# Third layer of a two-block feed-forward kernel with seven block products in place of eight, work moved between POOL, DVE and ACT, weights decoded ahead, inputs laid out as tiles

## The chip, the cores and the metric

The kernel runs on one core of one Trainium2 chip, as one program with one launch. The metric is the device time of that core in microseconds (us), the median of several executions. How the inputs are laid out on the host before the launch is not part of the time.

## The reference

```
x   = attention(q, k, v, cap)            # 4 batches, 12 heads, 448 tokens, head size 64
                                         # scores = cap * tanh(q k^T / 8 / cap), softmax over keys, times v
x   = x as (1792, 768)                   # 4 batches of 448 rows, 12 heads side by side
h   = max(x @ w1, x @ w2, x @ w3)        # layer 1: three 768 x 768 matrices
y   = h @ w_out                          # layer 2: 768 x 768
u   = sigmoid(y @ w_gate) * (y @ w_val)  # layer 3: two 768 x 1536 matrices
out = u @ w_out2                         # layer 4: 1536 x 768
```

The weights reach the kernel as 64-bit floats. The kernel rebuilds 32-bit floats from the two halves of each number ("decoding").

## The kernel before

**Precision.** A product of two 32-bit matrices is made of three TensorE passes: each factor is split into a high part (a cast to fp32r) and a low part (the factor less its high part), and high x high, low x high and high x low are summed in one PSUM bank. `product` (L78) does this for one 128-column block of a weight (six chunks of 128 rows) and one batch of 448 columns: 18 matmuls of 448 columns. The splits are one cast on ACT and one subtraction: `parts` (L60) for weights, on POOL as a rule; L245 and L246 for the attention output, L276 and L277 for layer 1, L288 and L289 for layer 2, L328 and L329 for layer 4.

**Weights.** `widths` (L46) decodes one block of 128 x 768 numbers: a DMA of 768 KB, an absolute value on ACT (L53), then four DVE operations (L54 to L57). `col_block` (L67) fetches or decodes a block and splits it. Layer 1 decodes 18 blocks while it works on batch 0 and keeps them in DRAM (`ws`) for the other three batches; six of the 18 are decoded early, one for each of pairs 1 to 6. Layers 2 and 3 decode each block when it is due. `layer3` also decodes the blocks of the last matrix into `ws2`.

**Order of the work.** 24 pairs of heads (six for each batch) go through attention. `load_pair` (L85) fetches a pair, `prepare` (L109) turns its queries and keys with eight transposes on TensorE (L116 to L120) and splits them, `Pair.scores`, `weigh` and `finish` do the rest. The loop at L464 issues, from pair 7 on, three layer 1 products for each pair, so that layer 1 of one batch runs beside attention of the next. When attention ends, 19 products of layer 1 are left; then come layer 2 (24 products), layer 3 (96 products: 12 column blocks, gate and value, four batches) and layer 4 (14 row tiles of 72 matmuls of 384 columns).

**Queues.** Every engine works through its own queue in order. The order of a queue is made by a planner that takes the program's order as priority and lets an operation go ahead of one that is not ready by its own model of the times. DMAs are issued by SP, but for a few.

**Engines.** Evacuations of PSUM are ACT's (L270, L288, L300) and DVE's (L272, L289, L303). POOL has the weight subtractions (L64), the first addition of the softmax sums for pairs 0 to 3 and from 13 on (L212, `adds` at L180), and most low parts of x and h.

Of the kernel before, what the change touches and what calls it, by code (L numbers as in the profile page):

```python
# [17 lines left out]
def tile_kernel(ctx: ExitStack, tc: tile.TileContext, q, k, v, cap, w1, w2, w3, wo, wg, wv, wo2, out):  # L18
    nc = tc.nc
    B, H, S, D = q.shape  # L20
    DM = wo.shape[1]
    DFF = wg.shape[1]
    P = 128
    NP = H // 2
# [5 lines left out]
    HALF = DM // 2  # L30

# [6 lines left out]
    hs = dram.tile([P, 2 * KC * S], F32, name="hs")  # L38
# [7 lines left out]
    def widths(wpool, src, shape):  # L46
        raw = wpool.tile([*shape, 2], I32, tag="wraw", name="wraw", bufs=2)
        dims = "p c f t -> p c (f t)" if len(shape) == 3 else "p f t -> p (f t)"
        nc.sync.dma_start(out=raw.rearrange(dims), in_=src.bitcast(I32))
        low, high = raw[..., 0], raw[..., 1]  # L50
        wf = wpool.tile(shape, F32, tag="wf", name="wf", bufs=2)
# [6 lines left out]
        return wf  # L58

# [7 lines left out]
    def col_block(wpool, w, j, keep=None, kept=False, sub=None):  # L67
        shape = [P, KC, P]
        if kept:
            wf = wpool.tile(shape, F32, tag="wf", name="wf", bufs=2)  # L70
            nc.sync.dma_start(out=wf, in_=keep)
        else:
            wf = widths(wpool, w[:, j * P : (j + 1) * P].rearrange("(c p) f -> p c f", p=P), shape)
            if keep is not None:
                nc.sync.dma_start(out=keep, in_=wf)
        return parts(wpool, wf, shape, sub)

    def product(ps, w, x):  # L78
        wh, wl = w
        passes = [(a, m, c) for a, ms in ((wh, (0, 1)), (wl, (0,))) for c in range(KC) for m in ms]  # L80
        for n, (a, m, c) in enumerate(passes):
            nc.tensor.matmul(ps, a[:, c, :], x[:, m, c, :], start=(n == 0), stop=(n == len(passes) - 1))  # L82


    def load_pair(n, pools):  # L85
        ld, wk, ep, pp, mm, (ident, ones, capb, tsc, kts, qts, vss, vts) = pools
        b, h0 = n // NP, 2 * (n % NP)
        qn = ld.tile([P, NT, 2, D], F32, tag="qn", name="qn")
        kn = ld.tile([P, NT, 2, D], F32, tag="kn", name="kn")
        vs, vx = vss[n % 4], vts[n % 4]  # L90
        kt, qt = kts[n % 2], qts[n % 2]
# [7 lines left out]
        nc.sync.dma_start(out=kn, in_=main(k))  # L99
        (nc.scalar if n == 0 else nc.sync).dma_start(out=qn, in_=main(q))  # L100
        for e in range(2):
            nc.sync.dma_start(out=kt[e * TAIL : (e + 1) * TAIL, e * D : (e + 1) * D], in_=rest(k)[e])
        nc.sync.dma_start(out=qt[:TAIL], in_=rest(q).rearrange("h p d -> p h d"))
# [3 lines left out]
        return qn, qt, kn, kt  # L107

    def prepare(n, loaded, pools):  # L109


        ld, wk, ep, pp, mm, (ident, ones, capb, tsc, kts, qts, vss, vts) = pools
        qn, qt, kn, kt = loaded
        kps, qps = (mm.tile([P, 512], F32, tag="mm", name="tr") for _ in range(2))
        for c in range(NT):
            nc.tensor.transpose(kps[:, c * P : (c + 1) * P], kn[:, c].rearrange("p h d -> p (h d)"), ident)  # L116
# [446 lines left out]
```

## Time and profile before

| what | us |
|---|---|
| median of three runs | 1116.49 (1116.25 to 1117.04) |
| the profiled execution's own time | 1115.94 |
| its span, first to last instruction | 1114.1 |
| TensorE busy in the span | 1089.5 (98%) |
| VectorE (DVE) busy | 515.9 (46%) |
| ScalarE (ACT) busy | 457.1 (41%) |
| GpSimd (POOL) busy | 251.9 (23%) |

The span falls into stages: attention of batch 0 (0 to 89.6 us), attention of batch 1 beside layer 1 of batch 0 with decoding (to 208), attention of batches 2 and 3 beside layer 1 (to 418.3), the rest of layer 1, layer 2 and layer 3 (to 932.9), layer 4 (to 1107.6), and the last copies and stores. A share over the whole span says little here, since the stages have different limits: the rows below go by stage. Busy time counts an operation from its start to its end; two operations of DVE that follow each other overlap by some 0.1 us, so that what an operation takes of DVE is better read from start to start.

### The profile page before, as it was taken

The numbers are of one execution on the slowest core, as the hardware profiler recorded it, in microseconds if no ns is written. First come the engines' busy times: TensorE is split into PE (matmuls) and PEld (weight loads), VectorE is DVE, ScalarE is ACT, GpSimd is POOL, SyncE is SP. The second block draws the span as 40 slices with busy tenths as digits, with TensorE's granted clock in tenths as the row PEclk, the third lists the DMA queues.
The fourth block names the chain that finished last, engine by engine and source line by source line (L and its number), as shares of the span: only waits on it lengthen the run. The fifth ranks groups of instructions, "written<-read, shape, count | busy, mean of one in ns | idle before, by whom it ended". The sixth has DMA issues, their size and how long they took to land.

```text
span 1114.1 us, 14715 instructions
## 1 busy us (share of the span) xinstructions
PE 1089.5 (98%) x5640; PEld 927.0 (83%) x5640; DVE 515.9 (46%) x835; ACT 457.1 (41%) x761; POOL 251.9 (23%) x165
## 2 busy tenths in 40 slices
PE   7989999999999999999999999999999999999997
PEld 4336676777777679999999999999999999999997
DVE  3997999624242431154342444444444433633331
ACT  6886667565655643333222212122222222433331
POOL 2200000354545455551110110111111114300000
PEclk9999999999999999999999999999999999999999
DMA  5576667834333115332130323233323212220010
GB/s 135 160 194 196 176 182 216 251 86 106 97 104 99 57 64 193 110 103 86 57 99 29 99 100 99 99 100 100 99 100 99 71 43 71 73 72 29 29 43 32
DMA packets 127247, 115.87 MB, mean 104 GB/s; under 512 B 70976, under 2 KB 111680, under 8 KB 127040
## 3 DMA queue, kind: packets, MB, share of 16 engines
q1 hardware_dynamic: 126096, 114.45, 33.6%
q8 instruction: 46, 0.75, 0.3%
q10 hardware_dynamic: 1072, 0.39, 0.1%
q14 instruction: 33, 0.27, 0.1%
HBM read 94.77 MB, written 20.05 MB: 103 GB/s over the span
## 4 chain that ended last, share of the span: by engine, by line
PE 87%; DVE 4%; ACT 4%; DMA 2%; issue 1%; POOL 0%; SPq 0%; ACTq 0%; DVEq 0%
PE mm L82 60%; PE mm L334 16%; PE pv L227 5%; PE sc L196 3%; DMA wraw<-in_moe_w_dram 2%; ACT e L209 2%; ACT e L201 2%; PE sc L193 1%; PE pv L229 1%; DVE sum L215 1%; PE tr L116 1%; PE tr L119 0%; DVE wf L57 0%; DVE wf L56 0%; DVE sum L217 0%
## 5 line engine op out<-in xcount | busy, mean ns | idle before, releaser
L64 POOL TENSOR_TENSOR wl<-wf,wh 128x768 fp32r<-128x768 f32 x84 | 156.9, 1868 | 595.8 <-PE mm L82 489.6
L82 PE MATMUL mm<-y,wh 128*128 128x448 f32 x1152 | 249.1, 365 | 0.0
L82 PEld LDWEIGHTS mm<-y,wh 128*128 128x128 f32 x1152 | 216.3, 188 | 17.1
L82 PE MATMUL mm<-x,wh 128*128 128x448 f32 x864 | 191.5, 370 | 2.5 <-ACT wh L63 1.3
L82 PEld LDWEIGHTS mm<-x,wh 128*128 128x128 f32 x864 | 159.5, 188 | 33.1 <-DVE ql L128 7.0
L63 ACT CAST wh<-wf 128x768 fp32r<-128x768 f32 x102 | 84.8, 832 | 195.9 <-PE mm L82 120.0
L334 PE MATMUL mm<-w,us 128*128 128x384 f32 x756 | 133.0, 334 | 0.0
L82 PE MATMUL mm<-y,wl 128*128 128x448 f32 x576 | 132.3, 365 | 0.0
L334 PEld LDWEIGHTS mm<-w,us 128*128 128x128 f32 x756 | 131.2, 188 | 0.0
L82 PEld LDWEIGHTS mm<-y,wl 128*128 128x128 f32 x576 | 108.2, 188 | 8.6
L53 ACT ACTIVATE wf<-wraw 128x768 f32<-128x768 f32 x60 | 54.2, 906 | 125.1 <-DMA wraw<-in_moe_w_val_dram 58.3
L329 DVE TENSOR_TENSOR us<-u,us 128x128 fp32r<-128x128 f32 (+1 forms) x192 | 63.4, 356 | 89.2 <-ACT us L328 88.5
L82 PE MATMUL mm<-x,wl 128*128 128x448 f32 x432 | 99.7, 366 | 0.0
L209 ACT ACTIVATE e<-e,capb 128x896 f32<-128x896 f32 x96 | 87.6, 949 | 0.8
L201 ACT ACTIVATE e<-sc,tsc 128x896 f32<-128x896 f32 x96 | 83.7, 908 | 10.1 <-PE sc L196 10.1
L82 PEld LDWEIGHTS mm<-x,wl 128*128 128x128 f32 x432 | 81.1, 188 | 7.0
L54 DVE TENSOR_SCALAR wf<-wf 128x768 f32<-128x768 f32 x60 | 33.3, 554 | 111.3 <-ACT wf L53 111.2
L328 ACT CAST us<-u 128x128 fp32r<-128x128 f32 (+1 forms) x192 | 49.5, 284 | 86.2 <-PE mm L334 83.0
L56 DVE SCALAR_TENSOR_TENSOR wf<-wraw,wf 128x768 int32<-128x768 int32 x60 | 79.4, 1324 | 1.8
L303 DVE TENSOR_TENSOR u<-mm,sg 128x448 f32<-128x448 f32 x48 | 29.8, 622 | 107.8 <-PE mm L82 107.8
L272 DVE TENSOR_TENSOR hm<-mm,hm 128x448 f32<-128x448 f32 x48 | 29.9, 623 | 106.1 <-PE mm L82 106.1
L227 PE MATMUL pv<-e,vs 128*64 128x448 f32 x288 | 68.7, 550 | 3.2 <-DVE r L237 2.2
(87 smaller groups left out, 1141.8 us busy)
## 6 DMA issues: line engine op xcount, KB each, us to landing
wf<-ws SPq DMA_DIRECT2D x72, 384.0 KB, 3.1
wraw<-in_moe_w_dram SPq DMA_DIRECT2D x18, 768.0 KB, 4.7
wraw<-in_moe_w_out_dram SPq DMA_DIRECT2D x18, 768.0 KB, 4.5
ws<-wf SPq DMA_DIRECT2D x30, 384.0 KB, 2.7
wraw<-in_moe_w_gate_dram SPq DMA_DIRECT2D x12, 768.0 KB, 4.3
wraw<-in_moe_w_val_dram SPq DMA_DIRECT2D x12, 768.0 KB, 4.8
kn<-in_k_dram SPq DMA_DIRECT2D x24, 192.0 KB, 3.8
vs<-in_v_dram SPq DMA_DIRECT2D x24, 192.0 KB, 3.1
```

The costliest lines, as they stand in the source:

```text
L53: nc.scalar.activation(wf, high.bitcast(F32), AF.Abs)
L56: nc.vector.scalar_tensor_tensor(wi, high, -0x40000000, wi, ALU.bitwise_and, ALU.bitwise_or)
L63: nc.scalar.copy(wh, wf)
L64: (sub or nc.gpsimd.tensor_sub)(wl, wf, f(wh))
L82: nc.tensor.matmul(ps, a[:, c, :], x[:, m, c, :], start=(n == 0), stop=(n == len(passes) - 1))
L196: nc.tensor.matmul(sc[:, j, :S], kk[own, c * P : (c + 1) * P], qq[own], start=(m == 0), stop=(m == 2))
L201: nc.scalar.activation(e, sc[:, :w, :S], AF.Tanh, scale=tsc)
L209: nc.scalar.activation(e, e, AF.Exp, scale=1.0 if self.general else capb)
L227: nc.tensor.matmul(self.pv[0][own, :S], lhs, e, start=(c == 0), stop=(c is None))
L328: nc.scalar.copy(us[:, 0, t, d], s)
L329: nc.vector.tensor_sub(us[:, 1, t, d], s, f(us[:, 0, t, d]))
L334: nc.tensor.matmul(pss[hf][:, :HALF], us[:, a, t, :], w2[fc][ww][:, hf * HALF : (hf + 1) * HALF], start=(fc == 0 and m == 0), stop=(fc == ...
```

## The change

**Layer 3** takes the blocks of weights two by two and the batches two by two (first 1 and 2, then 3 and 0) and computes the 2 x 2 product of blocks with seven block products in place of eight (the Winograd form of Strassen's scheme). A block product has three chunks, so nine matmuls of 448 columns. There are 24 groups ("quads"): two passes, six pairs of column blocks, gate and value; each has seven products, 168 in all. For each quad DVE makes four sums of weight blocks (384 wide), ACT makes seven casts, POOL five and DVE two subtractions (384 wide); after the products DVE makes seven additions (448 wide) that read PSUM, and for the value quads four multiplications. The u blocks go to DRAM (`us`) and come back for layer 4. The seven factors on the activations' side are made in `layer2_parts` for batches 1 and 2, and for batches 3 and 0 by hooks in layer 3: two splits and four groups of subtractions in quads 0 to 5, five splits of three chunks each in quad 11. Layer 2 works on batches 1 and 2 first, then on 3 and 0, with the same 24 products.

**Engines.** From pair 4 on, and in all of layer 1, what POOL did goes to DVE (weight subtractions, sums, low parts of x and h); the first evacuation of layer 1 goes from ACT to DVE. POOL comes back with layer 2.

**Decoding ahead.** `decode_ahead` handles the 42 blocks of layers 2 to 4 as a pipeline of three stages (fetch, decode, store), one step for each pair from pair 13, for every third product of the rest of layer 1, for each column block of layer 2 (12 steps) and for the first quads of layer 3. Up to near the end of layer 2 the decoded block lies in the one buffer of tag "s". Layers 2 to 4 fetch decoded blocks.

**Layout.** Queries and keys arrive turned (head size by tokens), so that the eight transposes of `prepare` go, and `kh`, `kl`, `qh`, `ql` are made from SBUF. Weights but the last matrix arrive as blocks whose rows of 6 KB lie together (before: runs of 1 KB).

```diff
-            self.adds = nc.vector if NP - 2 <= n <= 2 * NP else nc.gpsimd
+            self.adds = nc.vector if n >= NP - 2 else nc.gpsimd
...
-        for c in range(NT):
-            nc.tensor.transpose(kps[:, c * P : (c + 1) * P], kn[:, c].rearrange("p h d -> p (h d)"), ident)
-        nc.tensor.transpose(kps[:, NT * P : SK], kt, ident)
...
-        nc.scalar.copy(kh, kps[:, :SK])
+        nc.scalar.copy(kh, kf)
-        nc.vector.tensor_sub(kl, kps[:, :SK], f(kh))
+        nc.vector.tensor_sub(kl, kf, f(kh))
...
-                sub = None if kept else nc.vector.tensor_sub
+                sub = nc.vector.tensor_sub
...
-                        nc.scalar.copy(hm[i], ps[:, :S])
+                        nc.vector.tensor_copy(hm[i], ps[:, :S])
...
+    def decode_ahead(wpool, items, place):
+        raw, done = None, None
+        for src, shape, keep in (*items, (None,) * 3, (None,) * 3):
+            if done is not None:
+                nc.sync.dma_start(out=done[1], in_=done[0])
+            following = (raw_bits(wpool, src, shape), shape, keep) if src is not None else None
+            done = None
+            if raw is not None:
+                if place[0] == "s":
+                    t = wpool.tile([P, 3, HC, P], F32, tag="s", name="wd", bufs=1)
...
+                else:
+                    t = wpool.tile([P, DM], F32, tag="wf", name="wd", bufs=2)
...
+                done = decode(t, raw[0]), raw[2]
+            raw = following
+            yield
...
+        def prepare(self, upto=AHEAD):
+            while self.ready < min(upto, len(self.seq)):
...
+                if i == 6:
+                    t = self.wpool.tile([P, 3, HC, P], F32, tag="s", name="s", bufs=1)
+                    s1, s2, s4 = (t[:, e] for e in range(3))
+                    nc.vector.tensor_add(s1, a21, a22)
+                    nc.vector.tensor_sub(s2, s1, a11)
+                    nc.vector.tensor_sub(a21, a11, a21)
+                    nc.vector.tensor_sub(s4, a12, s2)
...
+                nc.scalar.copy(w[:, 0], src)
+                (nc.gpsimd if i in (1, 2, 4, 7, 3) else nc.vector).tensor_sub(w[:, 1], src, f(w[:, 0]))
...
+        def run(self, temps):
+            self.temps = temps
+            for n, (k, i) in enumerate(self.seq):
+                self.prepare(n + 1 + self.AHEAD)
...
+                self.after(k, i, ps)
+                for hook in self.hooks.get((k, i), ()):
+                    hook()
...
+            if m == 0:
+                nc.scalar.activation(t, t, AF.Sigmoid)
+            else:
+                nc.vector.tensor_mul(t, t, self.temp(k - 1, i))
+                nc.sync.dma_start(out=us[self.passes[n][0][i % 2], 2 * j + i // 2], in_=t)
...
+                if n > 2 * NP:
+                    next(ahead)
...
+            (half, 1): lambda: build(6, 10, t2),
+            (half, 2): lambda: build(7, 11, y0[:, tops]),
+            (half, 6): lambda: build(5, 12, y3[:, tops]),
+            (half, 7): lambda: build(4, 14, y3[:, ends]),
+            (half, 5): lambda: build(3, 13, y0[:, ends]),
```

## Rows read from the trace of the kernel before

**Rows 1.** The page, part 1 (busy time, share of the span, instructions) and the granted TensorE clock of part 2 in tenths of full speed.

```profile
PE 1089.5 (98%) x5640; PEld 927.0 (83%) x5640; DVE 515.9 (46%) x835; ACT 457.1 (41%) x761; POOL 251.9 (23%) x165
...
PEclk9999999999999999999999999999999999999999
```

**Rows 2.** The busy time by stretch: start and end in us, length, then for each engine the busy us and the number of instructions, the granted clock, the share of the DMA engines and GB/s.

```profile
0.00:58.00 58.00, 47.35 (x241) 23.45 (x241) 38.51 (x60) 42.35 (x54) 15.41 (x28) 1.00 0.60 156
58.00:89.60 31.60, 28.43 (x141) 12.47 (x141) 30.19 (x48) 26.22 (x34) 1.50 (x1) 1.00 0.67 179
...
109.92:209.32 99.40, 95.10 (x499) 70.62 (x497) 86.93 (x128) 66.81 (x93) 4.42 (x3) 1.00 0.67 197
211.07:403.90 192.83, 192.83 (x1029) 142.55 (x1030) 71.63 (x111) 115.64 (x162) 97.00 (x60) 1.00 0.34 98
418.32:932.88 514.56, 514.56 (x2539) 476.83 (x2540) 202.35 (x272) 129.89 (x196) 104.06 (x58) 1.00 0.28 91
932.88:1107.60 174.72, 174.72 (x1009) 174.43 (x1007) 67.90 (x192) 59.32 (x201) 20.49 (x11) 1.00 0.17 53
```

**Rows 3.** The chain of work that ended last, in order of time (start, length, what): one pair of the steady stage with what follows it, and the two last pieces.

```profile
383.72 0.33 PE tr L116 x3
...
384.59 3.16 PE pv L227 x16
...
388.50 7.63 PE mm L82 x36
...
418.32 514.56 PE mm L82 x2538
932.88 174.76 PE mm L334 x1008
```

**Rows 4.** TensorE in order of time: two score matmuls that recur once in a pair, five pairs apart (start, length).

```profile
109.92 0.47 PE L193 MATMUL sc<-qh,kh 128*128 128x448 f32 x1
...
209.32 0.47 PE L193 MATMUL sc<-qh,kh 128*128 128x448 f32 x1
```

**Rows 5.** TensorE and ACT in order of time at the program's start.

```profile
5.49 0.87 PE L116 MATMUL tr<-ident,kn 128*128 128x128 f32 x3 [5.49 <-DMA kn<-in_k_dram]
...
6.61 0.59 ACT L122 CAST kh<-tr 128x512 fp32r<-128x512 f32 x1 [3.85 <-PE tr L117]
...
8.24 1.11 PE L196 MATMUL sc<-qh,kh 64*128 64x448 f32 x4 [0.81 <-DVE qh L126]
```

**Rows 6.** DVE in order of time beside layer 1 of batch 0: one decoding (L54 to L57), then operations of 896, 768 and 448 columns.

```profile
106.89 0.56 DVE L54 TENSOR_SCALAR wf<-wf 128x768 f32<-128x768 f32 x1 [0.92 <-ACT wf L53]
...
109.07 0.96 DVE L57 SCALAR_TENSOR_TENSOR wf<-wraw,wf 128x768 int32<-128x768 int32 x1
109.94 1.08 DVE L212 TENSOR_TENSOR sum<-e 128x896 f32<-128x896 f32 x1
...
115.52 0.61 DVE L128 TENSOR_TENSOR ql<-tr,qh 128x448 fp32r<-128x448 f32 x1
116.05 0.61 DVE L244 TENSOR_TENSOR xn<-pv,xn 128x448 f32<-128x448 f32 x1
...
120.60 0.95 DVE L64 TENSOR_TENSOR wl<-wf,wh 128x768 fp32r<-128x768 f32 x1
121.46 0.95 DVE L56 SCALAR_TENSOR_TENSOR wf<-wraw,wf 128x768 int32<-128x768 int32 x1
```

**Rows 7.** POOL and then DVE in order of time near the end of layer 1: a POOL subtraction and the DVE operations beside it.

```profile
492.86 1.85 POOL L64 TENSOR_TENSOR wl<-wf,wh 128x768 fp32r<-128x768 f32 x1 [2.87 <-ACT wh L63]
492.90 2.62 DVE L56 SCALAR_TENSOR_TENSOR wf<-wraw,wf 128x768 int32<-128x768 int32 x1
495.45 0.61 DVE L272 TENSOR_TENSOR hm<-mm,hm 128x448 f32<-128x448 f32 x1
```

**Rows 8.** Lines of the kernel, each with its shortest, middle and longest instruction in ns, the first and last start in us, and the shape.

```profile
L56 DVE SCALAR_TENSOR_TENSOR wf<-wraw,wf x60: 942/959/2622, 32.6 to 904.2; 128x768 int32<-128x768 int32 x60
L303 DVE TENSOR_TENSOR u<-mm,sg x48: 611/625/626, 590.1 to 933.4; 128x448 f32<-128x448 f32 x48
L277 POOL TENSOR_TENSOR h<-hm,h x18: 1136/1153/1873, 224.6 to 500.2; 128x448 fp32r<-128x448 f32 x18
L329 DVE TENSOR_TENSOR us<-u,us x192: 210/291/1959, 911.6 to 1095.7; 128x128 fp32r<-128x128 f32 x144, 128x64 fp32r<-128x64 f32 x48
```

**Rows 9.** Groups of instructions by line, shapes kept apart or alone in their group (count, busy us, mean ns of one, idle before).

```profile
L64 POOL TENSOR_TENSOR wl<-wf,wh 128x768 fp32r<-128x768 f32 x84 | 156.9, 1868 | 595.8 <-PE mm L82 489.6
L56 DVE SCALAR_TENSOR_TENSOR wf<-wraw,wf 128x768 int32<-128x768 int32 x60 | 79.4, 1324 | 1.8
L329 DVE TENSOR_TENSOR us<-u,us 128x128 fp32r<-128x128 f32 x144 | 56.2, 401 | 81.4 <-ACT us L328 80.7 <-PE mm L334 0.8
```

**Rows 10.** DMA issues (count, KB each, median us from issue to landing), and who waited for whom longest (engine, line, releaser: us in total, times, longest).

```profile
wraw<-in_moe_w_out_dram SPq DMA_DIRECT2D x18, 768.0 KB, 4.5
ws<-wf SPq DMA_DIRECT2D x30, 384.0 KB, 2.7
kt<-in_k_dram SPq DMA_DIRECT2D x48, 16.0 KB, 3.0
...
ACT wf L53 <- DMA wraw<-in_moe_w_val_dram: 58.3, 10, 7.0
```

More of the change, by code (lines that the diff above doesn't have):

```diff
@@ L307, in layer4 @@
+    def layer4(ub, order, rooms, us_rooms, w2_rooms, mm, wpool, sm, rest):
         whole = [[(i, c) for c in range(NT)] for i in range(B)]
[L308 to L309 removed]
+        i0, i1, i2, i3 = order
+        tiles = whole[i0] + [((i0, i1), NT)] + whole[i1] + [((i2, i3), NT)] + whole[i2] + whole[i3]
         w2 = []
@@ L504, in compute @@
         for i, _ in enumerate(steps):
-            if i < KC:
-                part = slice(i * 2 * S, (i + 1) * 2 * S)
-                nc.sync.dma_start(out=flat(hb[0])[:, part], in_=hs[:, part])
+            if i < 2:
+                nc.sync.dma_start(out=f(hb[0][i]).rearrange("p a c s -> p (a c s)"), in_=hs[i])
+            if i % 3 == 0:
+                next(ahead)
         mm = Banks((*[six] * 6, mm, mm))
-        yb = [new_act2("y") for _ in range(3)] + [new_act("y")]
-        layer2(hb, yb, mm, wpool)
@@ L511, in compute @@
-        ushape = [P, NF, S]
-        ub = [act.tile(ushape, F32, tag="act", name="u") for _ in range(3)]
-        ub.append(new_act2("u", ushape, F32))
-        layer3(yb, ub, mm, wpool, sm)
-        layer4(ub, act, new_act2, mm, wpool, sm)
+        part = {i: rooms.half(n, "part") for i, n in {1: 10, 2: 11, 6: 12, 5: 13, 7: 14, 4: 15, 3: 2}.items()}
+        layer2_parts(hb[1], hb[2], part, rooms.chunks(3, "temp"), mm, wpool, sm, ahead)
+        later = {}
+        hooks = {}
+        l3 = Layer3((((1, 2), part), ((3, 0), later)), rooms, mm, wpool, hooks)
@@ new lines, in compute, with build @@
+        y3, y0 = y2 = [rooms.chunks(n, "y") for n in (0, 1)]
+        for j, _ in enumerate(layer2_plain((hb[3], hb[0]), y2, mm, wpool)):
+            next(ahead)
+            if j == KC - 2:
+                place[0] = "wf"
+                l3.start((3, 4, 5))
+        temps = [rooms.chunks(n, "temps") for n in (6, 7)]
+        t2 = [sm.tile([P, S], F32, tag="hm", name="t2") for _ in range(HC)]
+        tops, ends = slice(0, HC), slice(HC, KC)
+        def build(i, n, src):
+            later[i] = rooms.half(n, "part")
+            for c in range(HC):
+                split(later[i], c, src[c] if isinstance(src, list) else src[:, c])
@@ new lines, in compute, with fetch @@
+        for key, hook in at_.items():
+            hooks.setdefault(key, []).append(hook)
+        ub = {}
+        def fetch(b, ns):
+            ub[b] = [rooms.chunks(n, "u") for n in ns]
+            for i in range(2):
+                nc.sync.dma_start(out=ub[b][i], in_=us[b, i * KC : (i + 1) * KC].rearrange("c p s -> p c s"))
+        for k in range(2 * NF - 3):
+            hooks.setdefault((k, 3), []).append(lambda: next(ahead, None))
+        hooks.setdefault((NF + 1, 7), []).append(lambda: fetch(1, (0, 1)))
```

321 lines of the change are left out of this document (228 added, 93 removed).

## The prediction

> **What bounds the kernel now.** I read the page first. TensorE is busy for 1089.5 us of 1114.1 at full granted clock (1.00 in every stretch, its 2.4 GHz level) [rows 1, 2], so a gain must take work from TensorE, or time from the stretches in which it waits. The busy time by stretch shows which these are [rows 2]. From 418 us on, TensorE has no gap, and DVE is busy for 202 of 515 us; from 211 to 404, where attention runs beside layer 1, it has none either. Before 58 us ACT sets the pace (42 us busy, from about 11 us on), from 58 to 90 DVE does (30.2 of 31.6), and from 110 to 209 TensorE and DVE are both close to full. The chain of waits says the same: from 418.32 it is one piece of 2538 matmuls, then one of 1008 [rows 3]. Hence 514.56/2538 = 0.2027 us for a matmul of 448 columns, and 0.1734 for one of 384.
>
> **The change, part by part.**
>
> Layer 3: 96 products of 18 matmuls were 1728; 168 products of nine are 1512. 216 x 0.2027 = **-43.8**. Products follow each other without a gap in that one piece, whatever their number, so I put nothing on the starts of the 72 products more. Layer 3's own floor is 1512 x 0.2027 = 306.5, a quad 12.8.
>
> Transposes: eight of them take TensorE from 383.72 to 384.59, 0.87 us [rows 3]. The steady pair lasts 192.83/10 = 19.28, and would be 18.41 without them. What it becomes hangs on DVE. DVE's load in a steady pair is now 71.63/10 = 7.16. Durations are read from start to start [rows 6]: 0.53 for 448 columns, 0.86 for 768 (120.60 to 121.46), about 1.0 for 896 (1.08 less the 0.1 of overlap), and 3.05 for a decoding (106.89 to 109.94). A pair from 13 on gets one sum (1.0), three weight subtractions (2.58), three operations of 448 columns (1.59) and a decoding (3.05), so 15.4, or 84% of 18.41. The nearest row for such a pair is the stretch from 110 to 209: DVE 86.93 of 99.40 (87%), and 99.40/5 = 19.88 for a pair [rows 2, 4], which is 0.6 above the pair that TensorE alone allows. I take 0.4 of stretch at 84%, between 0 and 0.9 (at which nothing is gained): 18.8, so 12 x -0.47 = **-5.7**.
>
> The six pairs beside the decoding of layer 1 lose the same 0.87, but DVE rises from 17.39 to 17.9 by the evacuation that it takes from ACT. It is then 97% of TensorE's floor. Bounds: 18.4 and 19.9 (or 0.5 more, were DVE alone the limit). I take 19.4, nearer to the row: 6 x -0.48 = **-2.9**. What stands behind DVE's evacuation there is TensorE, since layer 1 has two banks.
>
> Start: the first score matmul starts at 8.24, after transposes that begin at 5.49 [rows 5]. Now `kh` is cast once the tail pieces of the keys have landed: issued by some 3.3 us, 3.0 to land [rows 10], 0.59 for the cast, so 6.9: **-1.3**. The first seven pairs keep what limits them (ACT's tanh and exp, DVE's decoding), so the transposes save between 0 and 7 x 0.87 = 6.1; I take **-1.5**, near the end at which they were hidden beside ACT.
>
> Decoding moved ahead: each step is 0.9 on ACT, 3.05 on DVE and two issues on SP. The pairs' share is in the sum above. In the rest of layer 1 and in layer 2, a step falls on three or on two products of 3.65; DVE has at most 3.05 + 5 x 0.53 = 5.7 of 7.3 there, and POOL 1.87 + 3 x 1.15 = 5.3 [rows 8, 9]. Cover enough: 0, at most +5. SP issues one DMA less in each pair for the layout, and two more for the step.
>
> Layout of the weights: 0. Landing of a block is 4.5 us for the blocks of the two output matrices, of which two thirds already lie in long runs [rows 10], and 1 us less would be hidden but for the first pairs.
>
> Layer 3 on DVE: this is the part that decides. A quad gives DVE four sums in a chain (384 columns, some 0.55 each by the slope between 448 and 768: 2.2), two subtractions (0.9), seven additions from PSUM (3.7), four multiplications in every second quad (1.06 on average), and a decoding in quads 0 to 11 (3.05): 10.9, or 7.9 without decoding. Hooks add 1.6 in quads 0 to 5 and 15 x 0.53 = 8 in quad 11. Against 12.8 this would just do. But POOL's five subtractions of 384 columns take 5 us of each quad (1.153 for 448 columns and 1.85 for 768 give 1.01). The trace shows what that does to DVE: a POOL subtraction starts at 492.86 and ends at 494.71; the DVE operation that starts 0.04 later, with two operands in SBUF, takes 2.62 in place of 0.96, and so ends 0.8 after POOL [rows 7, 8]. An addition that reads PSUM shows nothing of the kind: 611 to 626 ns over 48 of them [rows 8]. So sums, subtractions, multiplications and half of the decoding can be held, the seven additions can't.
>
> How much of POOL's 5 us is lost to DVE? Low bound: L56 exceeds its middle by 0.365 on average, 22 us over 157 us of POOL's weight subtractions, 14% [rows 8, 9]. High bound: all of it. In layer 4, L329 exceeds its middle of 0.29 by 0.11 on average, over 144 of them 16 us beside POOL's 20.5 [rows 2, 8, 9], which is 77%, but there DVE has hardly anything else. I take 40%, 2.0 a quad, since about half of DVE's work can be held. Then quads 0 to 5 need 14.5, which is 1.7 too much: 10 us. Quads 6 to 10 need 12.9: even. Quad 11 has 8 more, and quad 12 gives back 2.9. Weights are prepared four products ahead, 7.3 us of cover. 10 + 1 + 8 - 3 - 7 = **+9**. Bounds: 0 at 14%, and +49 at all of it (17.6 and 16.0 a quad, 29 + 19 + 8 - 7).
>
> The Trainium skill has a rule here (SBUF — State Buffer, section "Who interferes with whom"): a VectorE instruction with two SBUF inputs and a GpSimd instruction that reads SBUF exclude each other for a whole instruction, and VectorE instructions with at most one SBUF input outside the two-port modes don't contend. The rows on L56 and on the additions from PSUM agree. By the rule taken to the end, layer 3 pays the high bound, which is the second rival.
>
> Layer 4: the same 1008 matmuls. u comes back from DRAM; the last two batches are fetched after the first four row tiles, with three tiles of 72 x 0.1734 = 12.5 ahead of their first use, 37 us. 5.5 MB at the pace of a 768 KB block (4.5 us) take 32, and overlap: 0. If the cover went, some 10.
>
> Sum against the profiled execution: -43.8 - 5.7 - 2.9 - 1.3 - 1.5 + 9 = -46.2. Span 1114.1 - 46.2 = 1067.9, its own time 1115.94 - 46.2 = 1069.7; the median stands 0.55 above that execution, so **1070**.
>
> **The rivals.**
>
> 1. *TensorE stays the only limit.* Cast and sums are all covered, the lock costs nothing. 18.41 for all 18 pairs (-8.8 and -10.4), no stall in layer 3: 1116.5 - 43.8 - 19.2 - 1.3 - 1.5 = 1051, or 1046 with the first seven pairs. For it: DVE at 41% in layer 3 now, cover of four products. Against: the stretch of 0.6 that the busy pairs show.
>
> 2. *DVE becomes the bound of layer 3.* Each POOL subtraction keeps DVE out for its whole length: +49 in place of +9, 1110. For it: 2.62 for 0.96. Against: the 14%, and seven of DVE's operations that can go in between.
>
> 3. *The one buffer of the decoding makes the kernel slower.* Until the end of layer 2 a decoded block lies in one buffer, and ACT's first operation on the next block must wait for the store of the one before. ACT works in order, so tanh and exp of the pair stand behind that wait, then the scores, then TensorE. Price: a store of 2.7 behind a fetch of 4.5 [rows 10] is up to 7.2 in each of 12 pairs, +86, so 1156. It decides from (1116.5 - 1070)/12 = 3.9 us a pair. For it: ACT has stood up to 7.0 for such a fetch [rows 10]. Against: the store's data are ready a whole pair earlier, and ACT has 6.8 us to spare in a pair of 18.8 (11.56 now [rows 2], +0.9 for the step, -0.5 for the evacuation).
>
> That the seven products don't save their share can hardly be: a matmul of the same shape has cost the same in every layer.
>
> **How the numbers follow.** Forecast (1056 to 1085): 0.55. Rival 1: 0.2. Rival 2 (1086 to 1110): 0.18. Rival 3: 0.05, of it 0.04 slower. Something unseen: 0.02. The range of 8 in 10 takes in rival 1 and the near part of rival 2: 1048 to 1096. A difference under 0.2% (2.2 us) can't be told from no change here. Faster by more than that: 0.95; within: 0.01; slower: 0.04.
>
> **What would show it.** In the profile after, layer 3 should hold 1512 matmuls in about 315 us, with TensorE's gaps in quads 0 to 5 and around quad 12, ended by DVE; POOL's subtractions beside DVE operations of twice their length; pairs from 13 on at 18.8, the six before at 19.4; layer 2 at 87.5 and layer 4 at 174.8 without gaps. I am wrong if gaps in layer 3 sum to under 3 or over 25 us, if DVE isn't what ends them, if a pair from 13 on takes 19.2 or more, or if ACT waits for the store of the decoded block.

## The result and the profile after

| | us |
|---|---|
| before, median of the runs beside it | 1116.4 |
| after, median of 4 runs | 1073.92 (1071.26 to 1076.45) |
| ratio | 0.9618, 95% interval 0.9592 to 0.9645 |
| profiled execution of after: own time, span | 1076.45, 1074.7 |

The forecast was 1070, in a range of 1048 to 1096. The total is close in part by luck: attention gained some 7 us more than forecast, layer 3 and what follows lost some 14 more. The profiled execution is the slowest of the four, 2.5 over their median, and the parts below are its own. Of the kernel with the transposes back, below, one of four executions ran at a mean granted clock of 0.851 and took 1160.02; its figures are those of the other three.

The page of after, busy time and granted clock, answers to [rows 1]:

```profile
PE 1032.8 (96%) x5232; PEld 863.9 (80%) x5232; DVE 793.0 (74%) x1291; ACT 537.9 (50%) x947; POOL 218.6 (20%) x183
...
PEclk9999999999999999999999999999999999999999
```

TensorE gave up 56.7 us of work (1089.5 to 1032.8), the span 39.4 (1114.1 to 1074.7). The difference is new idle time. DVE has taken 277 us more.

The busy time by stretch of after, columns as in [rows 2]: five pairs of batch 1, eight steady pairs, layer 2, then layer 3 in five parts (to within quad 5, the end of quad 10 and quad 12, and two more), then layer 4.

```profile
103.77:200.44 96.67, 93.37 (x475) 67.16 (x473) 92.97 (x142) 66.09 (x87) 0.00 (x0) 1.00 0.65 218
237.03:383.38 146.35, 146.35 (x762) 107.06 (x761) 130.94 (x198) 99.40 (x132) 0.00 (x0) 1.00 0.62 198
...
476.40:563.90 87.50, 87.50 (x433) 81.11 (x432) 32.12 (x45) 34.72 (x58) 35.04 (x24) 1.00 0.38 123
563.90:640.00 76.10, 73.78 (x355) 66.16 (x355) 76.00 (x108) 32.93 (x66) 40.09 (x30) 1.00 0.50 165
640.00:717.00 77.00, 69.96 (x332) 60.99 (x331) 73.54 (x110) 31.35 (x66) 34.69 (x29) 1.00 0.53 176
717.00:742.80 25.80, 23.74 (x115) 21.21 (x114) 24.14 (x38) 13.30 (x29) 9.89 (x9) 1.00 0.43 138
742.80:795.00 52.20, 52.20 (x245) 47.37 (x246) 40.79 (x68) 22.27 (x45) 23.48 (x21) 0.97 0.53 182
795.00:891.00 96.00, 96.00 (x466) 87.17 (x466) 65.28 (x120) 40.20 (x91) 41.19 (x36) 1.00 0.26 82
896.70:1068.00 171.30, 171.28 (x987) 171.06 (x987) 60.74 (x187) 54.99 (x190) 11.07 (x6) 1.00 0.24 79
```

Read the DVE column against the length. A steady pair lasts 146.35/8 = 18.29, with DVE busy for 89% of it and TensorE without a gap. (The planner puts 13 decodings into these eight pairs, where the forecast counted one a pair.) In layer 3 DVE is busy for 76.00 of 76.10 us, then for 73.54 of 77, and there TensorE has gaps. Layer 2 holds its 87.5.

Layer 3 as the timeline of TensorE in after shows it (start, length, matmuls, and in brackets the gap ahead of the piece with what ended it):

```profile
563.91 3.81 PE L435 MATMUL mm<-part,ring 128*128 128x448 f32 x18
568.93 1.50 PE L435 MATMUL mm<-part,ring 128*128 128x448 f32 x6 [1.21 <-ACT ring L422]
571.08 65.98 PE L435 MATMUL mm<-part,ring 128*128 128x448 f32 x318 [0.66 <-DVE ring L423]
637.52 11.51 PE L435 MATMUL mm<-part,ring 128*128 128x448 f32 x54 [0.45 <-DVE temps L455]
...
684.22 2.06 PE L435 MATMUL mm<-part,ring 128*128 128x448 f32 x9 [1.70 <-DVE temps L455]
687.18 53.55 PE L435 MATMUL mm<-part,ring 128*128 128x448 f32 x258 [0.90 <-DVE temps L457]
742.80 149.32 PE L435 MATMUL mm<-part,ring 128*128 128x448 f32 x714 [2.06 <-DVE ring L423]
```

There are twelve gaps, 11.4 us in sum. DVE ended eleven of them, 10.2 us. Some 7 us lie in quads 6 to 8 (645 to 693); after quad 8 only the gap of 2.06 is left. But layer 3 takes 328.2 (563.9 to 892.1), which is 21.7 over its floor of 306.5. The other 10.3 lie inside the pieces: 65.98/318 = 0.2075 us a matmul and 149.32/714 = 0.2091, against the 0.2027 of before [rows 3]. Some 2 us of it belong to the gaps: the last matmul of a piece counts whole, 0.37 us, where the next would have begun after 0.20. No wait shows the rest; the section on the hardware comes back to it.

The decodings of layer 3, by their first operation on DVE (count, durations in ns, first and last start): there are nine, five of them up to 641.3 and the last in quad 8.

```profile
L60 DVE TENSOR_SCALAR wd<-wd x9: 546/562/1378, 594.7 to 678.6; 128x768 f32<-128x768 f32 x9
```

The start in after, from the timelines of ACT and TensorE, answers to [rows 5]: ACT loads its table only after its wait for the keys, where before it did so in idle time (at 1.48).

```profile
5.86 1.28 ACT L173 ACT_TABLE_LOAD   x1 [5.86 <-DMA kf<-in_k_dram]
7.16 0.62 ACT L173 CAST kh<-kf 128x512 fp32r<-128x512 f32 x1
...
7.83 0.74 PE L247 MATMUL sc<-qh,kh 64*128 64x448 f32 x2 [7.83 <-ACT kh L173]
```

Where the 39.4 us of the two spans lie, from the same marks in both traces (the score matmul of [rows 4], the first matmul of layers 2, 3 and 4, the end):

| part | forecast | measured |
|---|---|---|
| first score matmul, 8.24 to 7.83 | -1.3 | -0.4 |
| first seven pairs, to the mark at 82.40 / 80.12 | -1.5 | -1.9 |
| pair 7, 27.52 to 23.65 | -0.5 | -3.9 |
| pairs 8 to 12, 99.40 to 96.67 | -2.4 | -2.7 |
| pairs from 13 to the start of layer 2 | -5.7 | -9.7 |
| layer 2, 87.5 | 0 | 0 |
| layer 3, 350.2 to 328.2: fewer matmuls / gaps / slower pieces | -43.8 / +9 / 0 | -43.8 / +11.4 / +10.3 |
| layer 4 and the end | 0 | +1.3 |
| sum | -46.2 | -39.4 |

### The profile page after: what moved, and what is told of

Its sections match the earlier page's. It is cut to its first block, busy times and chain, and to the rows that moved or that the text cites. A ratio compares the mean times of both kernels' runs of the same rounds, so it can differ in the third digit from the quotient of the medians.

```text
span 1074.7 us, 15213 instructions
## 1 busy us (share of the span) xinstructions
PE 1032.8 (96%) x5232; PEld 863.9 (80%) x5232; DVE 793.0 (74%) x1291; ACT 537.9 (50%) x947; POOL 218.6 (20%) x183
## 5 line engine op out<-in xcount | busy, mean ns | idle before, releaser
L435 PE MATMUL mm<-part,ring 128*128 128x448 f32 x1512 | 316.8, 370 | 11.4 <-DVE temps L455 2.8
L435 PEld LDWEIGHTS mm<-part,ring 128*128 128x128 f32 x1512 | 283.8, 189 | 44.3 <-issue 9.2
L423 POOL TENSOR_TENSOR ring<-w,ring 128x384 fp32r<-128x384 f32 x96 | 115.8, 1213 | 172.5 <-ACT ring L422 130.6
L94 POOL TENSOR_TENSOR wl<-wf,wh 128x768 fp32r<-128x768 f32 x12 | 22.5, 1872 | 451.1 <-ACT wh L93 431.9
L94 DVE TENSOR_TENSOR wl<-wf,wh 128x768 fp32r<-128x768 f32 x72 | 68.4, 950 | 6.2 <-ACT wh L93 6.1
L422 ACT CAST ring<-w 128x384 fp32r<-128x384 f32 x96 | 48.3, 511 | 40.6 <-PE mm L435 29.6
L422 ACT CAST ring<-s 128x384 fp32r<-128x384 f32 x72 | 36.7, 510 | 60.9 <-DVE s L413 29.6
L140 PE MATMUL mm<-h,wh 128*128 128x448 f32 x288 | 62.3, 365 | 0.0
L59 ACT ACTIVATE wd<-wraw 128x768 f32<-128x768 f32 x42 | 38.1, 908 | 42.1 <-DMA wraw<-in_moe_w_out_dram 24.1
L472 ACT ACTIVATE temps<-temps 128x448 f32<-128x448 f32 x48 | 27.8, 578 | 60.8 <-DVE temps L452 23.0
```

The source lines that it names most:

```text
L94: (sub or nc.gpsimd.tensor_sub)(wl, wf, f(wh))
L140: nc.tensor.matmul(ps, a[:, c, :], at(x, m, c), start=(n == 0), stop=(n == len(passes) - 1))
L422: nc.scalar.copy(w[:, 0], src)
L423: (nc.gpsimd if i in (1, 2, 4, 7, 3) else nc.vector).tensor_sub(w[:, 1], src, f(w[:, 0]))
L435: nc.tensor.matmul(ps, w[:, wm, c, :], x[:, xm, c, :], start=(q == 0), stop=(q == len(order) - 1))
```

## The experiments

Three questions were open. Is it POOL that makes DVE late in layer 3? What is the absence of POOL in attention worth, and that of the transposes? And why are the pieces of layer 3 slower per matmul? Theory 1 is the forecast's account: POOL holds DVE in layer 3 ("hold" is the time by which POOL's operations lengthen DVE's), and elsewhere TensorE or DVE's own work sets the pace. Each text states its rivals.

**Layer 3 without POOL** (the low parts of five of seven weight factors are left out, and the high part is read in their place):

```diff
-                (nc.gpsimd if i in (1, 2, 4, 7, 3) else nc.vector).tensor_sub(w[:, 1], src, f(w[:, 0]))
+                if i in (6, 5):
+                    nc.vector.tensor_sub(w[:, 1], src, f(w[:, 0]))
```

> Starts from the changed kernel; leaves out POOL's five subtractions in each quad of layer 3 (the matmuls read the high part in place of the low part of those five factors), so TensorE, ACT and DVE have the same instructions and POOL has none in layer 3. Theory 1 (POOL's subtractions hold DVE's two-operand work for about 2 us a quad, and DVE is the bound of quads 0 to 12): DVE's sums and multiplications fall to their undisturbed length, quads 6 to 10 lose their gaps, layer 3 shrinks from 328 to 308 to 316 us, the kernel to 1054 to 1062. Theory 2 (DVE's own work is too much, the hold is a small part): layer 3 stays within 3 us of 328, the kernel at 1071 to 1076.

Measured: 1054.65, ratio 0.9444 (0.9428 to 0.9459). Timeline of TensorE, two stretches of layer 3, and the decodings between 563.7 and 640.3 (quads 0 to 5) in this kernel:

```profile
563.72 306.59 PE L436 MATMUL mm<-part,ring 128*128 128x448 f32 x1512
```

```profile
563.70:640.00 76.30, 76.30 (x378) 70.73 (x378) 74.47 (x134) 42.12 (x80) 0.00 (x0) 1.00 0.64 216
640.00:717.00 77.00, 77.00 (x382) 71.39 (x381) 59.88 (x110) 38.60 (x77) 0.00 (x0) 1.00 0.42 138
```

```profile
L60 DVE TENSOR_SCALAR wd<-wd x6: 551/552/561, 584.9 to 630.6; 128x768 f32<-128x768 f32 x6
```

All 1512 matmuls run in one piece at 0.2028. DVE is busy for 238.3 us in this layer, against 279.7 in after (the five rows of layer 3 summed), though its instructions are the same: 41 us are hold, 1.7 a quad, and by the excess of each operation over its undisturbed length 33 of them fall before 742.8, which is 2.6 a quad there. So POOL's subtractions cause the gaps. The slower pieces are gone too, but that doesn't tie them to POOL: below they come without POOL, and stay away with it. DVE's own work in quads 0 to 5, with six decodings, is 74.47 us in 76.30, so 12.5 a quad, as forecast.

**All subtractions on DVE**, nothing left out:

```diff
-                (nc.gpsimd if i in (1, 2, 4, 7, 3) else nc.vector).tensor_sub(w[:, 1], src, f(w[:, 0]))
+                nc.vector.tensor_sub(w[:, 1], src, f(w[:, 0]))
```

> Starts from the changed kernel; all seven subtractions of a quad's weights go to DVE, POOL has none in layer 3. DVE gets 5 x 0.46 to 0.55 = 2.3 to 2.8 us a quad more. Theory 1 (each quad loses 2 us of DVE to POOL): the hold goes, so that DVE's sum rises by 0.3 to 0.8 a quad: the kernel at 1074 to 1084. Theory 2 (the hold is small, under 0.7 a quad): DVE's sum rises by 2 a quad in quads 0 to 12, the kernel at 1095 or more.

Measured: 1065.66, ratio 0.9534 (0.9518 to 0.955), 8 us faster than after; theory 1 had expected it no faster. Timeline of TensorE in layer 3, and the decodings between 564.45 and 641.1 (quads 0 to 5):

```profile
564.45 156.42 PE L435 MATMUL mm<-part,ring 128*128 128x448 f32 x771
722.09 0.88 PE L435 MATMUL mm<-part,ring 128*128 128x448 f32 x3 [1.22 <-DVE ring L423]
727.30 154.13 PE L435 MATMUL mm<-part,ring 128*128 128x448 f32 x738 [4.33 <-ACT ring L422]
```

```profile
L60 DVE TENSOR_SCALAR wd<-wd x2: 553/554/556, 606.8 to 624.0; 128x768 f32<-128x768 f32 x2
```

The busiest quads, 0 to 5, have no gap with all subtractions on DVE. But the planner's order changed with the edit: two of the nine decodings begin there, where the kernel without POOL has six and after five. So DVE was not given 2.2 us a quad (five subtractions of 0.45, as in the forecast) on top of the same work: the four decodings moved later are 4 x 3.05/6 = 2.0 a quad. What the run shows is that 2.2 us of subtractions cost less than the hold of 2.6 that they replace, with part of the gain perhaps due to the order. Only what follows quad 11, with its five splits, makes TensorE wait (5.6 us). The first piece runs at 0.2029, the one after the gap at 0.2088, of which some 1.5 us (0.002 a matmul) are a lower granted clock at its start.

**Decoding earlier** (seven more steps before layer 3, four of them in layer 2 into tiles of their own; POOL stays), and **the same with all subtractions on DVE**:

```diff
-            if i % 3 == 0:
+            if i % 2 == 0:
...
+        spare = [rooms.flat(n, "wd", F32)[:, e * DM : (e + 1) * DM] for n in (4, 5) for e in range(2)]
...
+            if j < KC - 2:
+                place[0] = [spare.pop(0)]
+                next(ahead)
...
-        for k in range(2 * NF - 3):
+        for k in (6, 8, 10, 13, 15, 17):
```

> Starts from the changed kernel; POOL's subtractions stay, but seven more decoding steps are taken before layer 3 (every second product of the rest of layer 1, and two for each of four column blocks of layer 2, the second into tiles of their own, so that none waits for the one buffer), and the six left are put into quads 6, 8, 10, 13, 15 and 17. Theory 1 (DVE's total, its own work and the hold of 2.6 us a quad, makes the gaps): quads 0 to 5 need 8.4 + 1.6 + 2.6 = 12.6 of 12.8, quads 6 to 10 11 to 13.7; gaps of 4 to 9 us in place of 21.6, the kernel at 1057 to 1064. Theory 2 (the hold makes gaps by itself, whatever DVE's total): gaps of 15 or more, the kernel at 1067 or more.

> As e7_early, and all of a quad's subtractions on DVE (2.3 us a quad), POOL idle in layer 3. DVE needs 8.4 + 2.3 = 10.7 a quad, 12.3 in quads 0 to 5, 13.4 where a decoding falls, and 18.7 in quad 11. Theory 1: no gaps but at the start and at quad 11 or 12, layer 3 at 308 to 312, the kernel at 1054 to 1059. If gaps stay at 10 us as with the subtractions on DVE alone, they don't come from DVE's total.

Measured: 1066.69 (0.9552; 0.9533 to 0.9571) and 1060.49 (0.9482; 0.9447 to 0.9516). With POOL nine gaps are left within layer 3, 5.0 us in sum, inside theory 1's 4 to 9; eight of them lie in quads 2 to 5. That doesn't show what hold does without decoding: the planner moved all five decodings that were left back into quads 0 to 5 (572.7 to 640.8), though the program asks for them from quad 6 on. Without POOL one gap is left, ahead of the layer's first matmul, and yet the layer takes 7.7 us more than its floor. This profile is of the slowest of four executions, 1065.45; the fastest took 1054.78. Timeline of TensorE in the second kernel:

```profile
566.98 314.26 PE L437 MATMUL mm<-part,ring 128*128 128x448 f32 x1512 [1.78 <-ACT ring L424]
```

**Two steps of decoding for each block of layer 2, with the one buffer**:

```diff
-            next(ahead)
+            next(ahead, None)
+            next(ahead, None)
```

> Starts from the changed kernel; takes two decoding steps for each column block of layer 2 in place of one, so that layer 3 has no decoding (3.05 us of DVE a quad in quads 0 to 11). Theory 1 (DVE's total in quads 0 to 12, work and hold together, is what makes the gaps): without decoding quads 0 to 5 need 11.5 and quads 6 to 10 need 9.9 of 12.8, the gaps of quads 5 to 9 go, what is left is the start (2 us) and quads 11 and 12: layer 3 at 308 to 313, the kernel at 1055 to 1062; layer 2 stays at 87.5, its DVE goes from 37% to about 75%. Theory 2 (the gaps come from the order in which the weights are prepared, four products ahead, and not from DVE's total): layer 3 stays above 320, the kernel above 1066. Theory 3 (the steps only move: layer 2 gets the gaps): layer 2 grows by over 5 us.

Measured: 1081.46 (0.9691; 0.965 to 0.9732), slower than after. The waits of ACT in layer 2 of this kernel (in all, times, longest), and TensorE at the start of its layer 3:

```profile
ACT wd L59 <- DMA ws<-wd: 40.7, 10, 6.7
```

```profile
577.50 7.76 PE L436 MATMUL mm<-part,ring 128*128 128x448 f32 x27 [9.46 <-ACT ring L423]
592.10 303.00 PE L436 MATMUL mm<-part,ring 128*128 128x448 f32 x1485 [6.83 <-ACT ring L423]
```

This is the mechanism of the third rival: ACT stands for the store of the block before, and what is queued behind it on ACT, here layer 3's casts, comes late. In after it occurs as well, from 213 to 476 us nine times:

```profile
ACT wd L59 <- DMA ws<-wd: 7.1, 9, 3.2
```

There it costs TensorE nothing that shows: the pairs stay at 18.29 and layer 2 at 87.5. At twice the rate it does.

**DVE's share in attention.** First the twelve blocks of layer 1 that are decoded beside batch 0's products with three of their four DVE operations left out:

```diff
+        if light:
+            return wf
         nc.vector.tensor_scalar(wi, wi, 3, 0x3FFFFFF8, ALU.logical_shift_left, ALU.bitwise_and)
```

> Starts from the changed kernel; the 12 blocks that layer 1 decodes beside pairs 7 to 12 get only ACT's absolute value and the first of the four DVE operations (2.5 us of DVE less a block, 5 a pair); fetches, waits and the rest stay. In the changed kernel three of these pairs take 18.3 and three 21.4, 19.9 and 18.8. Theory A (DVE's share stretches them): all at 18.3, the stage 5 us shorter. Theory B (the fetch of the block does, ACT waits for it four times for 8.4 us): the stretched pairs stay within 0.5 us of what they were.

Measured: 1065.65 in one run. Six pairs, 8 to 13, of this kernel:

```profile
103.60:213.30 109.70, 109.70 (x570) 80.27 (x568) 86.49 (x135) 79.85 (x105) 0.00 (x0) 1.00 0.79 258
```

They take 18.28 each, where after needs 96.67 for five, with DVE busy for 96%: DVE's work is what stretches them. Then more load on DVE, additions of 448 columns tied to the data of pairs from 13 on, and, in a kernel before that, two free additions of 768 columns a pair:

```diff
+                    if n < B * NP:
+                        for _ in range(3):
+                            nc.vector.tensor_add(junk, pair.e[0][:, 0], pair.e[1][:, 0])
```

> Starts from the changed kernel; three more additions of 448 columns on DVE (1.6 us) in each pair from 13 on, which read that pair's exponentials, so that they can't be moved ahead of it. DVE's share there rises from 88% to 97%. Theory A (a pair is stretched once DVE is nearly full): 18.8 to 19.5 for a pair, 6 to 13 us in all. Theory B (the six pairs before were stretched by the blocks fetched and decoded just in time): 18.3 to 18.4 for a pair.

> Starts from the changed kernel; DVE gets two more additions of 768 columns (1.8 us) in each pair from 13 on, on a tile that nothing reads. A pair there takes 18.29 us at 88% of DVE, without a gap on TensorE; the pairs 7 to 12, at 96%, take 19.33. Theory A (a pair is stretched once DVE is nearly full): at 98% the pairs take 18.8 to 19.5, the kernel 1080 to 1088. Theory B (the six pairs are stretched by the blocks that are fetched and decoded just in time, not by DVE's share): the pairs stay at 18.3 to 18.4, the kernel within 3 us of 1074.

Measured: 1080.47 in one run, and 1082.62 (0.9697; 0.9674 to 0.9719). Tied additions left the first pairs at 18.29 and made five later ones 18.5 to 18.8. But DVE's share didn't rise to the 97% that the question needs: the planner took one decoding a pair in place of 13 in eight, and DVE was busy for 78.74 of 93.74 us, 84%, in the stretched pairs. So they are stretched by waits and not by a full DVE (ACT stood 18.9 us for DVE's L295 there), and a share doesn't tell which pair is stretched. The free additions miss their question: the planner put them between 9 and 149 us, so pairs from 13 on stayed at 18.29, and the early ones, where DVE has no room, paid.

**The transposes back on TensorE** (queries and keys in the layout of before; the code is that of L85 to L129 of before):

> The change without its new layout of queries and keys: they arrive as before and TensorE turns them with eight transposes a pair. Theory 1 (from pair 13 on TensorE is the only limit, 18.29 us a pair, so whatever TensorE does in a pair is paid in full): a pair from 13 on at 18.29 + 0.87 = 19.16, so 12 x 0.87 = 10.4 later at layer 2; the pairs 7 to 12, where DVE is at 96%, later by 0 to 0.87 each, up to 5; time 1084 to 1090. Rival (the transposes fill time in which TensorE waits): pairs from 13 on at 18.3 to 18.5, time 1073 to 1077.

Measured: 1103.72 (1097.76 to 1105.08; ratio 0.9865, 0.9832 to 0.9899), 30 us over after, where theory 1 had expected 10 to 16. Seven steady pairs of this kernel, and a wait between 233 and 400 us (in all, times, longest):

```profile
253.30:392.05 138.75, 136.66 (x724) 100.82 (x722) 122.98 (x184) 90.02 (x120) 0.00 (x0) 1.00 0.70 215
```

```profile
PEld mm L140 <- DVE kl L182: 6.7, 9, 0.8
```

A pair takes 138.75/7 = 19.82, with a shortest of 19.28: 0.99 over 18.29 is TensorE's share, and 0.5 more on average are waits. Nearly half of the 30 us lies ahead of that stage, where no run tells its cause apart: pair 13's last score matmul starts at 214.63 in place of 200.95, layer 3 at 592.96 in place of 563.91. The transposes write into the two banks that layer 1 uses, and DVE's subtraction L182 must read such a bank before the next product can have it.

**POOL and ACT back in attention and layer 1**, all that the change moved to DVE there:

```diff
-            self.adds = nc.vector if n >= NP - 2 else nc.gpsimd
+            self.adds = nc.vector if NP - 2 <= n <= 2 * NP else nc.gpsimd
-                sub = nc.vector.tensor_sub
+                sub = None if kept else nc.vector.tensor_sub
-                        nc.vector.tensor_copy(hm[i], ps[:, :S])
+                        nc.scalar.copy(hm[i], ps[:, :S])
-                split(hb[i][j // HC], j % HC, hm[i], nc.vector.tensor_sub)
+                split(hb[i][j // HC], j % HC, hm[i], (nc.gpsimd if kept else nc.vector).tensor_sub)
```

> The change, but in attention and layer 1 POOL and ACT keep what they had before: weight subtractions of the kept blocks, softmax sums from pair 13 on and the low parts on POOL, the first evacuation of layer 1 on ACT. Theory 1 (in pairs from 13 on DVE has room, 88% against about 55 to 60% here, and TensorE alone sets 18.29; in pairs 7 to 12 DVE is the limit and gets 3 x 0.5 us x 1/3 back): pairs from 13 on unchanged at 18.3, pairs 7 to 12 shorter by 0.1 to 0.5 each; time 1070 to 1076, no measurable difference from the change, or up to 3 us faster. Rival (POOL's instructions hold DVE, 157 us of them, and the chains through DVE lengthen the pair): pairs from 13 on at 18.6 or more, time 1078 or more.

Measured: 1133.08 (1.0149; 1.012 to 1.0177). It is slower than before, and 59 us over after: theory 1 is refuted here, and the rival's direction holds at several times its price. Five steady pairs, then POOL and DVE beside each other in one, then two waits between 233 and 400 us:

```profile
290.19:406.18 115.99, 98.58 (x476) 68.76 (x476) 93.35 (x95) 65.61 (x91) 57.80 (x30) 0.94 0.53 173
```

```profile
338.41 2.13 POOL L263 TENSOR_TENSOR sum<-e 128x896 f32<-128x896 f32 x1 [3.47 <-ACT e L260]
340.51 2.56 POOL L94 TENSOR_TENSOR wl<-wf,wh 128x768 fp32r<-128x768 f32 x1
...
338.62 2.74 DVE L62 SCALAR_TENSOR_TENSOR wd<-wraw,wd 128x768 int32<-128x768 int32 x1
341.40 2.49 DVE L63 SCALAR_TENSOR_TENSOR wd<-wraw,wd 128x768 int32<-128x768 int32 x1
```

```profile
ACT h L130 <- DVE hm L322: 36.3, 7, 5.5
...
PE sc L247 <- ACT e L252: 10.6, 7, 1.9
```

A pair takes 115.99/5 = 23.2. DVE is busy for only 80% of it, so its share isn't the limit. The decoding's operations last about as long as POOL's beside them (2.74 and 2.49 for 0.96), the maximum behind them (L322) comes late, ACT stands up to 5.5 us for it with tanh and exp behind, and the next scores wait for a bank that tanh must empty. Of the 24.5 us that these five pairs take over 5 x 18.29, TensorE is idle for 17.4; the other 7.1 are work at a lower clock, since the granted clock falls to 0.50 for a while after some of the gaps (0.94 on average in the row). The edit also puts the first evacuation of layer 1 back on ACT, and the run doesn't tell its part from POOL's. With DVE at 37% in the steady pairs of before [rows 2], the same POOL work cost no gap.

**Two gaps closed** in the kernel with earlier decoding and all subtractions on DVE (a copy of one column on ACT stands ahead of its wait for the keys, and layer 3's first two weight blocks are fetched into other buffers):

```diff
+    nc.gpsimd.memset(sq, 1.0)
+    nc.scalar.copy(sq, sq)
...
-                for e, tag in enumerate(("wh", "wl")):
+                for e, tag in enumerate(("wh", "wl") if k else ("wf", "wf")):
...
-        for k in (6, 8, 10, 13, 15, 17):
+        for k in (4, 6, 8, 10, 13, 15, 17):
```

> The kernel with earlier decoding and all of layer 3's weight subtractions on DVE (1060.5 measured), with two gaps closed: the first two weight blocks of layer 3 are fetched into other buffers, so that the fetch doesn't wait for the last product of layer 2 (1.78 us), and ACT does a one-column copy before its first wait for keys, so that its table load (1.28 us) lies ahead of that wait. Theory P (TensorE's slower pace in layer 3, 0.2078 against 0.2028 us a matmul, follows the gap at its start): without the gap layer 3 takes 306 to 308 us and the whole 1050 to 1055. Rival (the pace has another cause, such as the load on DVE's and the DMAs' side): layer 3 takes 313 to 316 without any wait, the whole 1056 to 1060. The first score matmul at 6.3 to 6.9 in either case.

Measured: 1053.98 (1053.26 to 1054.89), ratio 0.9445 (0.943 to 0.9461): with nothing left out, 20 us under after, and the fastest of all that compute the reference. Timelines of ACT and of TensorE, and the first quads of layer 3:

```profile
1.18 1.28 ACT L764 ACT_TABLE_LOAD   x1 [1.18 <-PEq L789]
...
6.29 0.74 PE L249 MATMUL sc<-qh,kh 64*128 64x448 f32 x2 [6.29 <-ACT kh L175]
...
562.98 306.59 PE L437 MATMUL mm<-part,ring 128*128 128x448 f32 x1512
```

```profile
562.98:640.00 77.02, 77.02 (x382) 71.37 (x381) 76.78 (x147) 38.25 (x77) 0.00 (x0) 1.00 0.41 138
```

Both edits did what was expected of the gaps (whether the pace hangs on the gap, as theory P has it, is taken up in the section on the hardware). DVE is busy for 76.78 of 77.02 us and TensorE doesn't wait once: a full DVE isn't a late one, as long as POOL leaves it alone and the ring of prepared weights covers four products.

**A gap on purpose** in the kernel without POOL in layer 3 (the same part left out), by 28 copies on ACT:

```diff
+                if (k, i) == (14, 1):
+                    for _ in range(28):
+                        nc.scalar.copy(src, src)
```

> The kernel without POOL in layer 3 (layer 3's low parts of five of seven weight factors left out, the high part read in place; 1054.65 measured, no gap in layer 3, pace 0.2028), with 28 copies of a weight block onto itself on ACT ahead of the first cast of quad 14, some 12 us of ACT against about 6 of free time, so that TensorE gets a gap of a few us there and nowhere else. Theory P (a gap makes the pace slower for the rest of the layer): after the gap, and after the granted clock is back at its upper level, 0.2078 to 0.209 us a matmul to the end of layer 3, some 4 us lost over 630 matmuls. Rival: 0.2028 again as soon as the clock is back, and the whole later by the gap and about 2 us at the lower clock level alone.

Measured: 1052.68 in one run, with 306.59 us for the 1512 matmuls in one piece. There was no gap, the copies found room on ACT; it says nothing on the question.

## Why the prediction came out right

Its direction and size held, and so did what it said of the gaps: 11.4 us, between 3 and 25, and DVE ended nearly all. Rival 2, the lock as the bound, had +49; rival 1 had none. By steps:

- **Layer 3's gaps, +9 against +11.4.** The mechanism was right, the size of hold too small in the busy quads (2.6 a quad against 2.0, some 8 us up to quad 12), and the number of decodings too large (a decoding in each of quads 0 to 11, where layer 3 has nine, the last in quad 8; three of 3.05 us are 9 us). DVE's own work beside a decoding, 12.5, was right. That the sum came near is in part luck: these two errors offset each other. Their place was half right: quads 1 to 5 have one gap, of 0.45, most lie in quads 6 to 8, where the last decodings are, and quad 12 has 2.06. The start of the layer, 1.9 us for a cast and a subtraction, was not in the sum.
- **"Products follow each other without a gap, whatever their number", with a floor of 306.5.** This is the step that failed. In the three longest pieces that followed a gap, 1290 of the 1512 matmuls, a matmul took 0.2075 to 0.2091. With the shorter pieces that is 10.3 us over the layer, of which some 2 are the restarts and some 1.7 a lower clock. The sentence under the rivals, that a matmul of the same shape has cost the same in every layer, doesn't hold in after.
- **The stretch of 0.4 in pairs from 13 on.** Wrong: DVE at 89% stretches nothing, 18.29 is TensorE's own time, and with the tied additions pairs were stretched at 84%. A share was the wrong measure. It was drawn from the pairs of before with DVE at 87%, and there the transposes shared layer 1's banks; the kernel with the transposes back shows waits for just those (19.82, L182). The gain of a transposed pair was also 0.99, not 0.87. So -9.7 in place of -5.7.
- **Pairs 8 to 12, 19.33 against 19.4.** Right, and for the stated reason: with less decoding they fall to 18.29.
- **Pair 7, -3.9 against -0.5.** No run tells its cause apart.
- **Start, -1.3 against -0.4.** ACT's table load moved behind the wait for the keys; a copy of one column ahead of that wait brings 1.54 (7.83 to 6.29).
- **POOL's work in attention handed to DVE**, counted only as load on DVE. It is what lets decoding ahead go free: with POOL back there, and ACT's evacuation with it, the change loses 59 us. The prediction knew the lock and applied it to layer 3 alone; it should have asked of the pairs, too, what POOL would do to a decoding that now stands beside it.
- **One buffer for the decoding, layouts, layer 2, layer 4.** Layer 2 and the layouts showed no cost, and layer 4 with the end took +1.3. But one of the forecast's signs of being wrong came true: ACT did stand for the store of the decoded block, up to 3.2 us, without a gap on TensorE. The third rival's mechanism was there, its price was not, until the rate was doubled.

The rule of the Trainium skill (SBUF — State Buffer, section "Who interferes with whom") that these instructions of VectorE and GpSimd exclude each other for a whole instruction agrees with 2.74 beside 2.13 and 2.56. That it didn't come to the high bound in after shows in the rows by line, where DVE's additions from PSUM (L457) go unharmed and the multiplications (L474) don't:

```profile
L423 POOL TENSOR_TENSOR ring<-w,ring x96: 1004/1124/2464, 562.9 to 873.7; 128x384 fp32r<-128x384 f32 x96
...
L474 DVE TENSOR_TENSOR temps<-temps x48: 609/618/1997, 591.5 to 896.7; 128x448 f32<-128x448 f32 x48
...
L457 DVE TENSOR_TENSOR temps<-mm,temps x24: 609/618/626, 578.5 to 889.8; 128x448 f32<-128x448 f32 x24
```

## What to carry to other kernels

Before work moves onto DVE beside POOL, ask of every stage, not only of the busiest, which of DVE's operations POOL can hold and who is queued behind them: the same POOL work cost no gap beside a DVE at 37%, and with it (and one evacuation on ACT) back beside a DVE that also decodes the kernel took 59 us more. A stage that keeps DVE full but POOL idle ran without a wait here, so it can be better to give DVE more work than to share it with POOL. And read the pace inside an uninterrupted piece (its length by its count) besides its gaps: nearly half of what layer 3 lost stood in no wait. Where a planner makes the order, look where the work went before an edit is read as moving one thing.

## What the hardware showed that was not expected

The pace of uninterrupted matmuls of 448 columns has two values. Middle and extreme durations in ns of layer 2's matmuls in after, and of the same matmuls in the kernel with POOL back in attention, both at a granted clock of 1.00 and without a gap:

```profile
L140 PE MATMUL mm<-h,wh x288: 362/365/369, 476.4 to 562.5; 128*128 128x448 f32 x144
```

```profile
L140 PE MATMUL mm<-h,wh x288: 368/368/368, 535.5 to 623.4; 128*128 128x448 f32 x144
```

The first takes 87.5 us, the second 89.3 for the same 432 matmuls, 2.0% more, with the same code and the engines beside it loaded alike or less (DVE 24 us against 32, ACT 34 against 35, POOL 35 in both). In layer 3 the three layers without a gap, at their start or inside, were fast (306.59 each), and the pieces that begin after gaps of 1.78 and 4.33 us were slow (314.26 and 154.13 above). But the piece after a gap of 6.83 was fast: 303.00 less some 1.6 for a granted clock of 0.50 over its first 3.3 us is 0.2030 a matmul. And two kernels whose edits leave the code of layer 3 alone, the one with free additions and the one with the lighter decoding, have the same two pieces with the other pace:

```profile
694.14 52.52 PE L435 MATMUL mm<-part,ring 128*128 128x448 f32 x258 [0.90 <-DVE temps L457]
```

```profile
736.56 144.96 PE L437 MATMUL mm<-part,ring 128*128 128x448 f32 x714 [3.08 <-DVE ring L425]
```

In after they took 53.55 behind the same 0.90, and 149.32 behind 2.06. POOL's subtractions are in all three, and the slow 314.26 had none. So neither POOL nor the length of a gap settles the pace, and a gap doesn't make it slow each time. That closing the gap of 1.78 brought 306.59 for 314.26 fits this, but an execution of the kernel with the gap took 1054.78 in all, as little as those without it (1053.26 to 1054.89). Why a piece falls into one or the other stays open.

Part of the loss is the clock. After the gap of 2.06 us in after, the granted clock falls (stretches of 1 us, columns as above):

```profile
743.00:744.00 1.00, 1.00 (x6) 0.92 (x6) 1.00 (x3) 0.68 (x2) 0.00 (x0) 0.95 0.99 340
744.00:745.00 1.00, 1.00 (x4) 0.91 (x3) 1.00 (x3) 1.00 (x3) 0.14 (x1) 0.50 1.01 349
...
748.00:749.00 1.00, 1.00 (x7) 0.91 (x6) 1.00 (x2) 0.00 (x0) 1.00 (x2) 1.00 0.74 278
```

It stands at 0.50, its level of 1.2 GHz, for some 3.5 us, which costs 1.75 us. That leaves (149.32 - 1.75)/714 = 0.2067 for the rest of that piece, the slow pace again. Behind the gap of 3.08 above it stayed at 1.00.
